# A fused recurrence and MLP kernel: the up product of four token chunks at once in 512 columns, running sums, and the mean of w_out taken off late

## Chip, cores, metric

One core of one Trainium2 chip. The metric is the device time of one execution in microseconds (us); a quoted time is the median of several executions.

## The reference, cut to what matters

A gated linear recurrence (4 batches, 8 heads, 768 steps, head size 48) makes 3072 token rows of 384; an MLP with d_ff = 1024 follows:

```python
# for each batch and head, over t
state = alpha[t][:, None] * state + outer(k[t], v[t])
y[t] = q[t] @ state
# x: (3072, 384) from y
h = x @ w_in                                  # (3072, 1024)
solu = h * softmax(h)
ln = (solu - mean(solu)) / sqrt(var(solu) + 1e-6) * g_ln
out = ln @ w_out                              # (3072, 384)
```

The weights come in float64, so the kernel also converts them. The kernels work without softmax's division: with u = h * exp(h), the layer norm cancels the scale but for the small epsilon, which needs the sum of exp and the sum of u squared of each token.

## The kernel before

Tokens are taken in chunks of 128. Four chunks, one per batch, make a group (128 steps of the recurrence); there are six groups. Attention of a group: `scores` (two halves, each into four PSUM banks), `masked` (DVE empties the banks), `read_state` and `read_values` (the product y), `next_state`. MLP of a chunk: `up`, `partial`, `down`, `finish`.

```python
def scores(g, half, a=None):
    a = a or banks("a", [NP, P])              # the same four PSUM banks each time
    ...
def masked(half, batches=range(B)):
    for b in batches:
        nc.vector.tensor_tensor(out=sT[:, b, ...], in0=a[b], in1=mask..., op=ALU.mult)

def up(n, half):                              # one chunk, half of d_ff
    h = ps_h.tile([P, HF, P], FP, tag="h", name="h")
    for f in range(HF):
        for a in range(KC):
            nc.tensor.matmul(h[:, f], lhsT=w_in[:, a, ...], rhs=d["xT"][:, a], ...)   # 128 columns
    nc.scalar.activation(out=d["e"][:, fs], in_=h, func=AF.Exp)
    nc.vector.tensor_tensor(out=d["u"][:, fs], in0=h, in1=d["e"][:, fs], op=ALU.mult)
    nc.scalar.activation(out=d["u2"][:, fs], in_=d["u"][:, fs], func=AF.Square)

for m in range(B, N + 1):                     # one chunk per turn
    ...                                       # up(m), a part of the next group's attention
        if s == 2:
            scores(g, 0); masked(0)
    ...
        if s == 3:
            read_begin(); read_state(0); read_state(1)
        if fall:
            down(m - 1, 0)                    # one chunk behind up
        if s == 3:
            read_state(2); read_state(3)
        if fall:
            down(m - 1, 1)
    ...
        if s == 2:
            scores(g, 1); masked(1)
```

## Time and profile before

| | before |
|---|---|
| median time | 430.35 us (428.69 to 430.63) |
| span of the profiled run | 427.6 us |
| mean granted clock of TensorE | 0.963 |
| stage A, to the first `up` of group 1 | 136.5 us |
| loop 1 (group 1's `up`, attention of group 2) | 57.1 us |
| three steady groups | 59.2, 59.0, 57.3 us |
| group 5 without attention, last `down`, tail | 44.0, 5.4, 9.1 us |

The stages are cut at the starts of `h` products in TensorE's timeline.

### The profile page before, as it was taken

How to read it: one execution, taken by the hardware profiler on the slowest of the kernel's cores; microseconds unless marked ns; L12 is line 12 of the kernel's file. 1: busy time of each engine (PE TensorE's matmuls, PEld its weight loads, DVE VectorE, ACT ScalarE, POOL GpSimd, SP SyncE). 2: the span in 40 equal slices, each digit the busy share in tenths (PEclk: the TensorE clock that was granted, in tenths of full speed). 3: DMA queues.
4: the chain of work that ended last, by engine and by line, in shares of the span. 5: the costliest groups of instructions: out<-in, count | busy, mean ns of one | idle time of the engine just before them, and what ended most of it. 6: DMA issues, size and time to landing. Idle time of an engine off the chain costs nothing.

```text
span 427.6 us, 12193 instructions
## 1 busy us (share of the span) xinstructions
PE 390.4 (91%) x5401; PEld 318.0 (74%) x5401; DVE 277.2 (65%) x480; ACT 144.3 (34%) x276; POOL 129.4 (30%) x142
## 2 busy tenths in 40 slices
PE   8667998598788989999999999999999999999992
PEld 8466897154667867878897797779788977977761
DVE  2869876899472998746976819976559863133331
ACT  0362776731105215252060522242420512222220
POOL 4100000004410566202772207561128723033330
PEclk9767999898899999999999999999999999999997
DMA  9976299530441933102844006651015000000010
GB/s 174 181 103 187 76 240 181 61 75 19 106 81 35 154 56 75 40 4 37 132 94 94 21 3 97 128 118 32 3 33 63 18 20 23 2 21 18 20 37 28
DMA packets 82047, 30.90 MB, mean 72 GB/s; under 512 B 60473, under 2 KB 80193, under 8 KB 81985
## 3 DMA queue, kind: packets, MB, share of 16 engines
q1 hardware_dynamic: 81536, 29.90, 35.4%
q8 instruction: 44, 0.72, 0.7%
q10 hardware_dynamic: 448, 0.14, 0.2%
q14 instruction: 19, 0.15, 0.1%
HBM read 25.30 MB, written 4.72 MB: 70 GB/s over the span
## 4 chain that ended last, share of the span: by engine, by line
PE 69%; DVE 16%; SPq 4%; DMA 4%; ACT 3%; issue 2%; ACTq 0%; POOL 0%; DVEq 0%
PE o L398 25%; PE h L346 24%; PE y L283 10%; PE a L251 5%; PE kv L325 2%; DMA raw<-in_moe_w_in_dram 2%; DVE aT L189 2%; SPq L138 2%; DVE u L352 2%; PE o L404 2%; SPq L160 1%; DVE low L497 1%; DVE top L493 1%; ACT w_out L516 1%; PE tp L270 1%
## 5 line engine op out<-in xcount | busy, mean ns | idle before, releaser
L346 PE MATMUL h<-xT,w_in 128*128 128x128 f32 x1152 | 135.4, 277 | 0.8 <-DVE u L352 0.7
L398 PE MATMUL o<-w_out,u 128*128 128x385 f32 x384 | 132.7, 496 | 2.7 <-ACT o_sb L426 2.1
L346 PEld LDWEIGHTS h<-xT,w_in 128*128 128x128 f32 x1152 | 130.8, 192 | 4.3 <-DVE u L352 1.5
L398 PEld LDWEIGHTS o<-w_out,u 128*128 128x128 f32 x384 | 71.3, 192 | 50.5 <-issue 3.1
L352 DVE TENSOR_TENSOR u<-h,e 128x512 f32<-128x512 f32 x48 | 33.1, 690 | 62.7 <-ACT e L351 62.7
L424 POOL TENSOR_TENSOR r<-sums,mhalf 128x1 f32<-128x1 f32 x24 | 13.3, 553 | 147.4 <-DVE sums L420 147.4
L351 ACT ACTIVATE e<-h 128x512 f32<-128x512 f32 x48 | 28.5, 593 | 84.0 <-PE h L346 83.9
L353 ACT ACTIVATE u<-u 128x512 f32<-128x512 f32 x48 | 30.2, 630 | 74.1 <-DVE u L352 74.1
L212 POOL TENSOR_TENSOR kT<-kT,hT 128x1024 f32<-128x1024 f32 (+1 forms) x10 | 18.4, 1859 | 89.0 <-DVE kT L164 89.0
L262 DVE TENSOR_TENSOR sT<-a,mask 128x512 f32<-128x512 f32 x44 | 27.5, 683 | 17.4 <-PE a L251 17.4
L361 POOL TENSOR_TENSOR part_e<-e 128x512 f32<-128x512 f32 x20 | 30.1, 1506 | 14.0 <-ACT e L351 14.0
L251 PE MATMUL a<-qv,kT 32*128 32x128 f32 x704 | 27.0, 301 | 5.8 <-DVE least L202 3.2
L251 PEld LDWEIGHTS a<-qv,kT 32*128 32x128 f32 x704 | 24.7, 209 | 7.6 <-issue 4.0
L426 ACT ACTIVATE o_sb<-o,r 128x384 f32<-128x384 f32 x24 | 14.0, 582 | 44.4 <-POOL r L424 44.4
L283 PE MATMUL y<-sT,vn 128*32 128x128 f32 x768 | 24.5, 284 | 2.7 <-issue 2.6
L313 ACT COPY xT<-y 128x384 f32<-128x384 f32 x24 | 11.4, 479 | 43.5 <-PE y L283 43.5
L189 DVE TENSOR_TENSOR_SCAN aT<-aT,seed 128x516 f32<-128x516 f32 x18 | 25.3, 1407 | 0.6
L283 PEld LDWEIGHTS y<-sT,vn 128*32 128x32 f32 x768 | 21.7, 114 | 4.0 <-issue 3.2
L334 DVE TENSOR_TENSOR state<-state,kv 128x512 f32<-128x512 f32 x8 | 5.5, 687 | 25.9 <-PE kv L325 25.9
L361 DVE TENSOR_TENSOR part_u<-u 128x512 f32<-128x512 f32 x20 | 15.0, 749 | 11.1 <-ACT u L353 11.1
L189 DVE TENSOR_TENSOR_SCAN hT<-aT,unit 128x516 f32<-128x516 f32 x18 | 20.9, 1214 | 0.1
L283 PE MATMUL y<-qv,state 32*32 32x128 f32 x1280 | 19.0, 278 | 1.6 <-issue 1.6
(114 smaller groups left out, 456.3 us busy)
## 6 DMA issues: line engine op xcount, KB each, us to landing
an<-in_alpha_dram SPq DMA_DIRECT2D x24, 192.0 KB, 5.1
kn<-in_k_dram SPq DMA_DIRECT2D x24, 192.0 KB, 4.6
qn<-in_q_dram SPq DMA_DIRECT2D x24, 192.0 KB, 4.6
out_dram<-o_sb SPq DMA_DIRECT2D x24, 192.0 KB, 1.9
vn<-in_v_dram SPq DMA_DIRECT2D x24, 128.0 KB, 3.6
raw<-in_moe_w_out_dram SPq DMA_DIRECT2D x8, 384.0 KB, 3.9
raw<-in_moe_w_in_dram SPq DMA_DIRECT2D x16, 128.0 KB, 4.4
vn<-in_v_dram SPq DMA_DIRECT2D x24, 64.0 KB, 3.5
```

Of the source, the lines that this page charges most:

```text
L189: nc.vector.tensor_tensor_scan(out=o, data0=a, data1=s, initial=1.0, op0=ALU.mult, op1=ALU.add)
L212: nc.gpsimd.tensor_tensor(out=kT[:, part], in0=kT[:, part], in1=hk[:, part], op=ALU.mult)
L251: nc.tensor.matmul(a[b][:, i], lhsT=kT[quarter(b), kb], rhs=qv[quarter(b), qb], start=kb == h, stop=kb != h, tile_position=(32 * b, 0), sk ...
L262: nc.vector.tensor_tensor(out=sT[:, b, half * NP : half * NP + NP], in0=a[b], in1=mask[:, None, :].to_broadcast([P, NP, P]), op=ALU.mult,)
L283: nc.tensor.matmul(y_bank(b)[quarter(r), a], lhsT=lhsT, rhs=rhs, start=(b, r) not in begun, stop=stop, tile_position=(row, 32 * r), skip_g ...
L346: nc.tensor.matmul(h[:, f], lhsT=w_in[:, a, (f0 + f) * P : (f0 + f + 1) * P], rhs=d["xT"][:, a], start=(a == 0), stop=(a == KC - 1),)
L351: nc.scalar.activation(out=d["e"][:, fs], in_=h, func=AF.Exp)
L352: nc.vector.tensor_tensor(out=d["u"][:, fs], in0=h, in1=d["e"][:, fs], op=ALU.mult)
L353: nc.scalar.activation(out=d["u2"][:, fs], in_=d["u"][:, fs], func=AF.Square)
L361: eng.tensor_tensor(out=t, in0=d[key][:, 0:HF], in1=d[key][:, HF:FC], op=ALU.add)
L398: nc.tensor.matmul(o[:, 0 : DM + 1], lhsT=d["u"][:, f], rhs=w_out[:, f], start=(f == 0), stop=(f == FC - 1), skip_group_check=True,)
L426: nc.scalar.activation(out=o_sb, in_=d["o"][:, 0:DM], func=AF.Copy, scale=r)
```

## The change

The intent: `up` of a group's four chunks as one product of 512 columns, so 48 records per group where there were 48 per chunk, and a quarter of the weight loads; sums over d_ff as running adds of 512 columns instead of trees; sums over partitions by small products in 32-column squares; the mean of w_out is no longer subtracted before the first `down`, but added to the output for group 0 and taken off w_out on POOL during group 1. Since `u` of a group is complete only after eight steps, `down` trails `up` by a whole group. The core of the diff:

```diff
-    def up(n, half):
-        ...
-                nc.tensor.matmul(
-                    h[:, f], lhsT=w_in[:, a, (f0 + f) * P : (f0 + f + 1) * P], rhs=d["xT"][:, a],
+    def up(g, f):
+        h = ps_h.tile([P, T4], FP, tag="h", name="h")
+        for a in range(KC):
+            nc.tensor.matmul(
+                h, lhsT=w_in[:, a, f * P : (f + 1) * P], rhs=d["x"][:, a].rearrange("p b t -> p (b t)"),
...
+    def running(g, f):
+        for i, eng in enumerate((nc.gpsimd, nc.vector)):
+            p = d["p"][:, i]
+            eng.tensor_tensor(out=p, in0=d[0][i] if f == 1 else p, in1=d[f][i], op=ALU.add)
...
+    def centre(f):
+        nc.gpsimd.tensor_tensor(out=w_out[:, f, 0:DM], in0=w_out[:, f, 0:DM], in1=mean_sb, op=ALU.add)
...
+    todo = [(3, 0), (3, 1)]
+    for g in range(1, G + 1):
+        for s in range(FC):
+            if rise:
+                up(g, s)
...
+                elif s == 6:
+                    masked(0)              # first scores were issued in step 5
...
+            if rise and s:
+                running(g, s)
...
+            if todo:
+                n, half = todo.pop(0)
+                down(n, half)              # chunks of the group before
+            if more:
+                if s == 5:
+                    scores(g + 1, 0)
+                elif s == 6:
+                    scores(g + 1, 1)
+                elif s == 7:
+                    masked(1)
+                    read_begin()
+                    for i in range(4):
+                        read_state(i)
+                    read_values(g + 1)
+                    next_state(g + 1)
```

The first stage is rebuilt as well: the weights come in eight pieces into slots that later hold `u`, alpha of group 0 is transposed on TensorE, and ScalarE checks the range of pieces 2 and 3 ahead of the first exp.

## The prediction

> **What bounds the kernel now.** I read the page first, then the chain of waits in order of time, then busy time by stretches, then the timeline of one group of four chunks. From the page (busy tenths in 40 slices, then two rows of the costliest groups):
>
> ```profile
> PE   8667998598788989999999999999999999999992
> DVE  2869876899472998746976819976559863133331
> L346 PE MATMUL h<-xT,w_in 128*128 128x128 f32 x1152 | 135.4, 277 | 0.8 <-DVE u L352 0.7
> L398 PE MATMUL o<-w_out,u 128*128 128x385 f32 x384 | 132.7, 496 | 2.7 <-ACT o_sb L426 2.1
> ```
>
> TensorE (PE) is full from slice 16 on, some 160 us into the span; before that VectorE (DVE), the weight conversion and the loads share the limit. Each fp32 matmul is two records (576 products, 1152 records). The stretches show it as one row each (length, PE busy, weight-load busy, DVE, ACT, POOL):
>
> ```profile
> 48.00:84.00 36.00, 28.80 (x398) 23.67 (x396) 26.68 (x54) 26.80 (x69) 0.00 (x0) 0.95 0.76 155
> 136.00:160.00 24.00, 22.13 (x176) 18.81 (x165) 21.95 (x27) 6.59 (x12) 12.25 (x10) 1.00 0.64 107
> 193.65:252.84 59.19, 59.19 (x893) 48.96 (x893) 41.71 (x67) 19.42 (x33) 24.16 (x25) 1.00 0.35 69
> ```
>
> The last row is a steady group: 59.2 us, PE never idle, full clock. What it is made of stands in the chain (start, us, what):
>
> ```profile
> 193.65 5.56 PE h L346 x48
> 199.21 5.19 PE o L398 x16
> 204.73 5.46 PE h L346 x48
> ...
> 217.09 5.36 PE h L346 x48
> 222.45 2.00 PE a L251 x64
> 224.45 5.38 PE o L398 x16
> 230.17 2.00 PE a L251 x64
> 232.17 5.55 PE h L346 x48
> ...
> 247.30 3.63 PE y L283 x128
> 250.93 1.91 PE kv L325 x96
> ```
>
> Each chunk's `up` is 48 records, each `down` 16, and between `o` and the next `h` 0.33 us go by (204.40 to 204.73): the two small sum products of L404. Between the two `a` blocks lie 5.7 us of other PE work, and the timeline shows what they hide:
>
> ```profile
> 225.50 2.48 DVE L262 TENSOR_TENSOR sT<-a,mask 128x512 f32<-128x512 f32 x4
> 232.18 2.48 DVE L262 TENSOR_TENSOR sT<-a,mask 128x512 f32<-128x512 f32 x4 [2.82 <-PE a L251]
> 235.14 0.60 ACT L351 ACTIVATE e<-h 128x512 f32<-128x512 f32 x1 [8.88 <-PE h L346]
> 235.77 0.69 DVE L352 TENSOR_TENSOR u<-h,e 128x512 f32<-128x512 f32 x1 [1.10 <-ACT e L351]
> 236.49 0.63 ACT L353 ACTIVATE u<-u 128x512 f32<-128x512 f32 x1 [0.76 <-DVE u L352]
> ```
>
> Emptying the four banks of scores costs DVE 2.5 us, and it starts at once because nothing stands ahead of it.
>
> [...] 5.46/48 = 114 ns for 128 columns, 5.19/16 = 324 ns for 385, a slope of 0.82 ns per column and little fixed cost. So wide columns buy little. [...] in the trace the loads of `h` are about 113 ns each, hidden but just as long as the 128-column product. [...] the trace has the 256-column partial sums of DVE at 0.42 us alone and 1.28 us beside POOL[...].
>
> **The change part by part, steady group.**
> - `up`: 48 records of 512 columns, 324 + 127 x 0.82 = 428 ns each, 20.6 us, against 5.56 + 5.46 + 5.36 + 5.55 = 21.9. Gain 1.3 us per group.
> - Sums: four gaps of 0.33 go (1.3 us); sixteen small column-tiled matmuls of 64 columns come, 32 records at 28 ns (3.63/128 of `y`) = 0.9 us. Gain 0.4.
> - DVE and POOL trees become seven adds of 512 (0.75 and 1.5 us each): 5.3 against 9 us on DVE, 10.5 against 12 on POOL. Off the path, worth nothing by themselves.
> - Work left on PE: `up` 20.6, `down` 8 x 2.6 = 20.8, attention 14.6 (transposes 1.4, scores 4.0, read 7.3, new state 1.9), sums 0.9, switching 0.6: 57.5 against 59.1.
> - **Order**, from the instruction order of the built kernel. Attention of the next group is squeezed into eight steps. Step 6 is up, down (5.2 us), then the second scores, which want the four banks of the first scores back. On DVE their masking now stands behind that step's `u`: after the end of `up` come exp 0.6, `u` 0.7, three small operations 0.6 and masking 2.5 = 4.4 us, with only a `down` of 2.6 to hide it: PE waits 1.8. Step 7 is worse: masking stands behind the last running sum too: 0.6 + 0.7 + square 0.6 + add 0.8 + 2.5 = 5.2 against 2.6: PE waits 2.6 before the read. The first scores wait about 0.6 more on ScalarE (the split queries, then three copies of 0.5). Together 5 us: a steady group of 62.5 for 59.2.
>
> **Stage by stage.**
> A, to the first `up` of group 1 (before: about 136). The three first loads are all in 192-byte pieces and land near 20.2 as now. Values are issued behind 32 weight transfers instead of 16, at about 37, so the first read begins near 40 (now 36.8). ScalarE must then check pieces 2 and 3 before the first exp; their 32 issues at 0.42 to 0.54 us end near 50, landing 3 to 4 us later, so `u` of step 0 is at about 57. Then PE has six `up` at 2.6 and eight array sums at 4 x 0.43 = 1.7 us (no longer four in parallel, 13.8 against 6.3 us in all): 29 us, to 86. DVE goes on from the last `u` (about 83): 2.5 + 2 x 4.1 of conversion, group 1's transposes and scans 15, finishes 2, queries and POOL 5 to about 115, then scores, masks, read and state 18.5: A = 133. Centring (3.8 us on DVE now) is off this path.
> B, loop of group 1, with only one chunk's `down` to fill in. DVE before the first scores: wait 3.2, four `u` 3, transposes 3 x 3.1, scans 9, sums 2.3, finish 1.1 = 28, then POOL and ScalarE 5: 33; after it 2 + 2.6 + 3.9 + 2 + 2.6 + 5.2 + 7.3 + 1.9 = 27.5. B = 60, with PE work of 41.
> C, three steady groups: 187.5. D, group 5 without attention: 20.6 + 20.8 + 1 = 42.5. E, the last four chunks' `down`, which now trail by a whole group: 21.8. Tail as now: 427.6 less 418.5 = 9.
> Sum 133 + 60 + 187.5 + 42.5 + 21.8 + 9 = 454 of span, and 2.7 more for the measured median (430.35 against 427.6) gives 457. I take off 4, since hand scheduling stacks waits: **453 us**.
>
> **The rivals.** (1) The waits at steps 5 to 7 don't bind, because masks get in earlier than I count, and the start is as short as its lighter DVE work suggests. For: conversions shrink from 70 operations to 40, and centring leaves DVE. Then C loses 15, A perhaps 8: 430, about the same. Against: the order on DVE is fixed in the build. (2) B overlaps too, with PE at its work of 41: then PE-bound throughout, some 412 to 418, faster. Against: DVE rows in the start of B add up to 28 us before any score. (3) Loads bind longer, ScalarE's check of piece 3 stalls the first exp past 60, and clocks fall in the gaps of A and B: 465 to 470. For: the row of 37 to 48 us has a granted clock of 0.84.
>
> **Range and chances.** The trailing `down` (E with PE idle in B, some 18 us) I hold nearly certain, the waits in C likely (four fifths), A is good to 8 us either way. Range 432 to 468. Faster by over 2% needs nearly all idle time gone: 0.06; within 2% needs half of it gone: 0.14; slower 0.80.
>
> **What would show it.** Right: records of `h` with 512 columns near 430 ns back to back; a steady group of 61 to 64 us, with PE idle 1 to 3 us before the second scores and before the read, released by the masking on DVE; group 1's loop near 60 us with PE busy about 41; a last stretch of only `down`, 21 us; first exp after 50 us. Wrong: a steady group under 59 us with PE full, or group 1's loop under 50, or a first stage under 125 us.

## More of the kernel before

The lines that show what bounds it are in the prediction. One more row of the page matters later: the clock granted to TensorE in 40 slices of the span, in tenths (9 is 90% or more).

```profile
PEclk9767999898899999999999999999999999999997
```

After the first stage the clock is at 90% or more in every slice until the tail.

## The result, and the profile after

502.68 us (501.21 to 503.66, 4 runs) against 430.49 us (428.69 to 431.47): a ratio of 1.168, 95% interval 1.163 to 1.173. A ratio is always the mean time of one kernel's runs over the mean of the other's runs of the same rounds, so it is not quite the ratio of the medians. Executions over 1.5% slower than the fastest of the same kernel are left out of the means. Slower was predicted, but the time lies far above the range of 432 to 468.

| stage | before | predicted | after |
|---|---|---|---|
| A, to first `up` of group 1 | 136.5 | 133 | 150.6 |
| B, loop 1 | 57.1 | 60 | 71.2 |
| C, three steady groups | 175.5 | 187.5 | 207.1 |
| D, group 5 without attention | 44.0 | 42.5 | 42.6 |
| E, last `down` | 5.4 | 21.8 | 21.6 |
| tail | 9.1 | 9 | 8.4 |
| span | 427.6 | 454 | 501.6 |

D, E and the tail are right within 0.6 us. A, B and C together are 48 us over. Busy tenths and clock of the kernel after, from its page:

```profile
PE   9738399584889818699989899898899897999993
PEclk9879599797789977799989899988999998999998
```

The clock row has dips all along, in the steady groups too, where the kernel before had none. Two rows of the costliest groups (count, busy us, mean ns, idle before):

```profile
L350 PE MATMUL h<-x,w_in 128*128 128x512 f32 x288 | 136.2, 611 | 9.6 <-DVE slot L357 9.6
...
L256 PE MATMUL a<-qv,kT 32*128 32x128 f32 x704 | 40.2, 343 | 26.1 <-POOL qv L232 17.0
```

The wide product costs what the 1152 narrow records of before cost (135.4 us there). The scores, though not touched by the change, went from 27.0 to 40.2 us busy. The stretches (length, PE busy, weight loads, DVE, ACT, POOL, then the granted clock) of loop 1, a steady group, and the last `down`:

```profile
150.80:221.83 71.03, 51.05 (x685) 31.68 (x685) 39.47 (x48) 17.96 (x30) 30.30 (x25) 0.86 0.25 49
...
291.18:360.73 69.55, 63.90 (x765) 38.90 (x765) 41.14 (x60) 19.97 (x33) 22.61 (x20) 0.95 0.28 58
...
471.60:493.24 21.64, 21.59 (x96) 12.56 (x96) 2.68 (x15) 2.33 (x4) 2.20 (x4) 1.00 0.10 37
```

A steady group has 63.9 us of PE "busy" for work that the prediction put at 57.5. So the work itself was slower, and that shows in TensorE's timeline (start, us, what, idle before it and who released it):

```profile
319.14 2.74 PE L350 MATMUL h<-x,w_in 128*128 128x512 f32 x6
321.72 2.76 PE L423 MATMUL o<-w_out,slot 128*128 128x385 f32 x8
326.66 4.33 PE L256 MATMUL a<-qv,kT 32*128 32x128 f32 x64 [2.18 <-POOL qv L232]
...
336.37 3.75 PE L256 MATMUL a<-qv,kT 32*128 32x128 f32 x64
...
348.15 3.81 PE L288 MATMUL y<-qv,state 32*32 32x128 f32 x184 [0.20 <-DVE sT L267]
352.38 1.08 PE L288 MATMUL y<-qv,state 32*32 32x128 f32 x66 [0.41 <-issue]
353.39 1.95 PE L288 MATMUL y<-sT,vn 128*32 128x128 f32 x62
355.83 2.04 PE L288 MATMUL y<-sT,vn 128*32 128x128 f32 x65 [0.49 <-issue]
...
359.56 1.17 PE L330 MATMUL kv<-vn,kg 128*32 128x64 f32 x34 [0.79 <-issue]
```

The waits stand where the prediction had them: before the first scores on the queries, inside the second scores (3.75 us for 2.0 of work, at a clock of 1.00: it is fed bank by bank as the masks empty them), and before the read on `sT`. Three things the prediction did not have: the first scores take 4.33 us after their wait, 184 records of the read take 3.81 us, and there are gaps called "issue", in which TensorE waits for nothing that the profile shows (0.41, 0.49 and 0.79 us here). The same table of stretches, for the two slow blocks, gives the cause of the first two:

```profile
326.66:330.90 4.24, 4.24 (x64) 3.84 (x64) 2.40 (x2) 1.72 (x4) 3.58 (x3) 0.60 0.69 160
...
348.10:352.00 3.90, 3.81 (x184) 3.18 (x184) 0.00 (x0) 0.00 (x0) 0.00 (x0) 0.59 0.02 4
```

The granted clock is 0.60 and 0.59; over the 33 us of the same group ahead of the wait it is 1.00. Cut into finer stretches, the clock is 0.50 from 327.8 to 330.2 and from 348.15 to 351.0; with the partly slow slices at the ends, each is by estimate about 3.4 us at half speed (for the first, 4.24 us at 0.60 come to 4.24 x 0.40 / 0.50).

It does not come each time. In the third steady group of the same run the first scores ran at full clock (1.00) behind the same wait:

```profile
396.22 2.71 PE L256 MATMUL a<-qv,kT 32*128 32x128 f32 x64 [2.20 <-POOL qv L232]
```

That group is also the shortest of the three (69.3, 69.5 and 68.2 us).

DVE's side of the waits, in the same group:

```profile
335.54 2.48 DVE L267 TENSOR_TENSOR sT<-a,mask 128x512 f32<-128x512 f32 x4
...
345.01 0.69 DVE L368 TENSOR_TENSOR p<-p,u 128x512 f32<-128x512 f32 x1 [0.70 <-ACT u L358]
345.62 2.48 DVE L267 TENSOR_TENSOR sT<-a,mask 128x512 f32<-128x512 f32 x4
```

The first scores end at 330.99, their masks start 4.6 us later, behind the next `u`; the second masks start after the running sum. That is the order the prediction described.

In stage A, the first exp came at 56.4 and was held by the range check of piece 3, as predicted, and TensorE then ran slowly (clock 0.62 from 57.7 to 62.3):

```profile
57.76 4.54 PE L350 MATMUL h<-x,w_in 128*128 128x512 f32 x6 [9.62 <-DVE slot L357]
```

### The profile page after: what moved, and what is told of

Read it like the earlier page. It is cut to its first block, busy times and chain, and to the rows that moved or that the text cites. A ratio compares the mean times of both kernels' runs of the same rounds, so it can differ in the third digit from the quotient of the medians.

```text
span 501.6 us, 10779 instructions
## 1 busy us (share of the span) xinstructions
PE 417.8 (83%) x4705; PEld 250.4 (50%) x4705; DVE 262.2 (52%) x410; ACT 147.0 (29%) x251; POOL 127.7 (25%) x124
## 4 chain that ended last, share of the span: by engine, by line
PE 40%; DVE 24%; issue 4%; ACT 3%; POOL 2%; DMA 1%; SPq 0%; DVEq 0%; ACTq 0%; POOLq 0%
PE h L350 12%; PE o L423 10%; PE y L288 9%; PE a L256 6%; DVE sT L267 4%; DVE aT L193 4%; DVE p L368 3%; DVE hT L193 3%; DVE slot L357 3%; PE kv L330 2%; DVE kT L168 2%; ACT e L356 2%; POOL qv L232 1%; DVE least L207 1%; POOL qe L232 1%
## 5 line engine op out<-in xcount | busy, mean ns | idle before, releaser
L350 PE MATMUL h<-x,w_in 128*128 128x512 f32 x288 | 136.2, 611 | 9.6 <-DVE slot L357 9.6
L423 PE MATMUL o<-w_out,slot 128*128 128x385 f32 x384 | 136.7, 503 | 3.6 <-DVE o_mean L441 3.6
L423 PEld LDWEIGHTS o<-w_out,slot 128*128 128x128 f32 x384 | 74.3, 196 | 61.2 <-issue 20.8
L350 PEld LDWEIGHTS h<-x,w_in 128*128 128x128 f32 x288 | 54.3, 195 | 72.9 <-issue 51.9
L357 DVE TENSOR_TENSOR slot<-h,e 128x512 f32<-128x512 f32 x48 | 33.0, 688 | 110.0 <-ACT e L356 110.0
L256 PE MATMUL a<-qv,kT 32*128 32x128 f32 x704 | 40.2, 343 | 26.1 <-POOL qv L232 17.0
L358 ACT ACTIVATE u<-slot 128x512 f32<-128x512 f32 x48 | 30.3, 630 | 65.5 <-DVE slot L357 65.5
L368 POOL TENSOR_TENSOR p<-p,e 128x512 f32<-128x512 f32 x30 | 40.1, 1336 | 33.0 <-ACT e L356 32.8
L368 DVE TENSOR_TENSOR p<-p,u 128x512 f32<-128x512 f32 x30 | 30.3, 1011 | 8.4 <-ACT u L358 8.4
L288 PEld LDWEIGHTS y<-qv,state 32*32 32x32 f32 x1280 | 22.0, 126 | 22.7 <-DVE sT L267 15.6
```

Of the source, the lines that this page charges most:

```text
L256: nc.tensor.matmul(a[b][:, i], lhsT=kT[quarter(b), kb], rhs=qv[quarter(b), qb], start=kb == h, stop=kb != h, tile_position=(32 * b, 0), sk ...
L288: nc.tensor.matmul(y_bank(b)[quarter(r), a], lhsT=lhsT, rhs=rhs, start=(b, r) not in begun, stop=stop, tile_position=(row, 32 * r), skip_g ...
L350: nc.tensor.matmul(h, lhsT=w_in[:, a, f * P : (f + 1) * P], rhs=d["x"][:, a].rearrange("p b t -> p (b t)"), start=(a == 0), stop=(a == KC ...
L357: nc.vector.tensor_tensor(out=u, in0=h, in1=e, op=ALU.mult)
L358: nc.scalar.activation(out=u2, in_=u, func=AF.Square)
L368: eng.tensor_tensor(out=p, in0=d[0][i] if f == 1 else p, in1=d[f][i], op=ALU.add)
```

## The experiments

Theory after the result: (a) a longer wait of TensorE can cost twice, once as the wait and once as slower work behind it, because the granted clock falls (0.60 and 0.59 in the two blocks above, 1.00 over the 33 us ahead of the first); (b) long unbroken runs of narrow records end in issue gaps (0.41 to 0.79 us above); (c) `down` trailing by a group leaves idle time in loop 1 and 21.6 us alone at the end. The rivals: the wide product itself is slow; the start is to blame; what is repaired in one place is lost in the next.

### e1: masks issued right behind their scores

```diff
                 if s == 5:
                     scores(g + 1, 0)
+                    masked(0)
                 elif s == 6:
                     scores(g + 1, 1)
+                    masked(1)
                 elif s == 7:
-                    masked(1)
                     read_begin()
```
(and the old `masked(0)` of step 6 goes)

> The changed kernel with one thing moved: each masking of the four score banks is issued right behind its scores, ahead of the next step's u and running sum on DVE. Theory (the waits at steps 6 and 7 come from the order on DVE[...]): the waits of 1.7 and 2.7 us before the second scores and the read vanish in the three steady groups, the read's first half goes from 3.8 back to 1.9 us, so a steady group falls from 69.5 to about 63, group 1's loop from 71 to about 63, the whole from 502.7 to about 475 us. Rival (the masks only expose the next wait, u and the running sum being late instead): a steady group stays above 67, the whole above 492.

Measured 479.79 us, ratio 1.114 (1.106 to 1.121); 475 was expected. Steady groups fell from 69.0 on average to about 65. The second scores take 2.07 us again and the read starts at once at a clock of 1.00; what stays is the wait before the first scores, with slow scores (clock 0.59) behind it, and a longer gap in the read:

```profile
312.34 4.23 PE L256 MATMUL a<-qv,kT 32*128 32x128 f32 x64 [2.18 <-POOL qv L232]
...
333.46 1.08 PE L288 MATMUL y<-qv,state 32*32 32x128 f32 x66 [1.51 <-issue]
```

So the order of the masks on DVE was worth 23 us: 12 in the three steady groups, and 10 in loop 1, which ends after 61.2 us instead of 71.2. In the steady group shown the two mask waits came to 4.4 us; with them went the slow clock behind the read's wait (1.1), and the longer issue gap gave 1.1 back.

### e2: products on constants in front of the three waits

```diff
+                    warm(40 if g == 1 else 9, ps_h, "h")
                     scores(g + 1, 0)
...
+                    warm(14 if g == 1 else 7, ps_h, "h")
                     scores(g + 1, 1)
...
+                    warm(18 if g == 1 else 11, ps_h, "h")
                     read_begin()
```

> The changed kernel with throwaway 128-column products of ones put into PE's waits before the first scores, the second scores and the read (9, 7 and 11 of them in a steady group; 40, 14 and 18 in group 1's loop). They shorten no wait. Theory[...]: the scores after the wait go from 4.3 to about 2.1 us and the read's first half from 3.8 to about 1.9, a steady group from 69.5 to about 65.5, group 1's loop from 71 to about 63, whole about 482 us, mean granted clock of the stretches 1.00. Rival (scores and read are slow after a wait for another cause, such as their operands or small tiles): nothing but added work, 500 to 508 us.

Measured 498.19 us, ratio 1.159: most of the expected gain was missed. The fillers did their work where they stood (first scores 2.69 instead of 4.33 us), but the read, now without a pause in front of it, ran into a longer issue gap, and the clock fell there:

```profile
347.25 1.05 PE L288 MATMUL y<-qv,state 32*32 32x128 f32 x62 [1.80 <-issue]
348.23 5.37 PE L288 MATMUL y<-sT,vn 128*32 128x128 f32 x128
```

The clock in the stretch of the second line was 0.68, and the block takes 3.70 us in the kernel before. Behind the gap of 1.51 us in e1 the clock stayed at 1.00. Filling all waits alike moved the loss here; it did not remove it.

### e3: range checks of pieces 2 and 3 behind the first exps

```diff
-    in_range(2)
-    in_range(3)
...
         if f % 2:
+            if p < 4:
+                in_range(p)
```

> The changed kernel with ScalarE's range checks of weight pieces 2 and 3 moved behind the first exps of group 0. Theory (the first exp, at 56.4 us, waits on ScalarE behind a check that waits for piece 3 to land at 54.5): first exp near 46 us, the first up of group 1 at about 141 instead of 150.6, whole about 493 us. Rival (conversion on DVE waits for the same piece anyway): the first exp moves but the end of the first stage by less than 3 us, whole 499 to 503.

Measured 494.05 us, ratio 1.148: as expected, 8.6 us less. The first exp comes at 45.2 us, and the first `up` of group 1 starts at 143.5 instead of 150.6 (141 was expected), and the steady groups stay at 69.

### e4: the wide product cut into four of 128 columns

```diff
-        for a in range(KC):
-            nc.tensor.matmul(h, lhsT=w_in[:, a, ...], rhs=d["x"][:, a].rearrange("p b t -> p (b t)"), ...)
+        for b in range(B):
+            for a in range(KC):
+                nc.tensor.matmul(h[:, b * P : b * P + P], lhsT=w_in[:, a, ...], rhs=d["x"][:, a, b], ...)
```

> The changed kernel with each up of 512 columns done as four products of 128 columns, all else alike: undoes the width alone. Theory (width is worth 0.15 us a step, 48 steps, less what lies in waits): 3 to 7 us slower than the changed kernel, about 507. Rival (narrow products are bound by their weight loads, so width is worth more): 515 or more. Rival (width is worth nothing on the path): within 1 us.

Measured 506.61 us, ratio 1.180 (1.171 to 1.188). By the medians that is 3.9 us slower, as expected, but it is not clear of the spread: the runs overlap (503.28 to 509.82 against 501.21 to 503.66), and the two profiled runs have nearly the same span (501.4 and 501.6 us). The trace shows the width itself: an `up` with its `down` takes 5.27 us from one to the next in this form and 5.17 us in the wide one. Over 46 steps 0.1 us would be some 4 us, by estimate; in the profiled run it was made up in the steady groups, where the waits before the first scores are shorter (1.83 to 1.90 us) and two of the three were not followed by slow scores. The wide product is not what made the kernel slow: without it the kernel is no faster.

### e5: e1, and the read split around the last `down`

```diff
+            if more and s == 7:
+                read_begin()
+                read_state(0)
+                read_state(1)
             if todo:
                 n, half = todo.pop(0)
                 down(n, half)
...
                 elif s == 7:
-                    read_begin()
-                    for i in range(4):
-                        read_state(i)
+                    read_state(2)
+                    read_state(3)
```

> The kernel with early masks (e1), and besides the read of the old state split in two around the down of step 7, as the kernel before has it. Theory (the gaps marked 'issue', 1.5 us after some 190 records of the read in a row and 0.5 us twice later[...]): the 1.5 us gap goes, a steady group falls from 65 to 62 to 63.5 us, the whole from 479.8 to about 472. Rival (the gaps belong to the read's operands or banks, wherever it stands): same gaps, 478 to 482.

Measured 472.95 us, ratio 1.100 (1.092 to 1.108): as expected. This is how the kernel before had it. The two halves of the read:

```profile
321.77 1.90 PE L288 MATMUL y<-qv,state 32*32 32x128 f32 x128
...
326.40 1.91 PE L288 MATMUL y<-qv,state 32*32 32x128 f32 x128
```

No gap is left inside them; in e1 the same 256 records had a gap of 1.51 us after the 190th. In the sums of waits "y on issue" falls from 10.1 us in e1 to 4.1.

Where the gaps fall can be counted. In the group of the changed kernel shown above, 66 + 62 = 128 records of TensorE lie between the gap at 352.38 and that at 355.83. Counted over the timelines of all runs from 40 us on, after the first such gap each "issue" gap (0.2 to 1.9 us) lies 128 records behind the one before it, or a multiple of 128 less at most five. So the gaps come at a count of records, not at a certain length of run; by that count e5 has a point in the second half of the read too, and with the `down` shortly before it no gap shows there. No run isolated what makes the gaps; why they come is not shown.

### e6: e1, and the state's decay on POOL moved from step 3 to step 6

```diff
-                    decay(g + 1)          # step 3, ahead of the queries on POOL
...
                     scores(g + 1, 1)
                     masked(1)
+                    decay(g + 1)          # step 6
```

> The kernel with early masks (e1), and besides the decay of the state on GpSimd (4.1 us in step 3, beside the scans on DVE) put off to step 6. Theory (PE's wait of 2.2 us before the first scores, and the half clock of those scores after it, come from the scans and sums on DVE and the queries on GpSimd being drawn out by each other): the second pass of scans falls from 8.0 to about 6 us, the wait goes, the scores take 2.1 instead of 4.2 us, a steady group falls from 65 to about 61.5, the whole to about 468. Rival (the wait is DVE's own row of work, GpSimd has nothing to do with it): wait stays above 1.5 us, 477 to 481.

Measured 471.76 us, ratio 1.095; 468 was expected. The wait before the first scores halves, and the clock holds at 1.00:

```profile
307.31 2.68 PE L256 MATMUL a<-qv,kT 32*128 32x128 f32 x64 [1.05 <-POOL qv L232]
```
```profile
306.20:310.00 3.80, 2.74 (x66) 2.38 (x65) 0.91 (x3) 2.81 (x6) 3.72 (x4) 1.00 0.82 198
```

The clock is 1.00 in that stretch, 0.59 in e1's (312.3 to 316.5). Taking 1.1 us from the wait took 1.6 us more from the scores behind it (e1's line of the same group is shown there). This is the clearest pair for point (a): same records, same order on TensorE, 4.23 against 2.68 us. The second scans of that group on DVE took 1.97, 1.23 and 1.23 us; in the changed kernel, with the decay still in step 3, 1.97, 1.39 and 2.04.

### e7: all repairs together

e5 and e6 and e3; values loaded ahead of the second weight piece; ScalarE's copies of the array sums ahead of one weight piece's work; group 1's keys turned back before `finish` and decay in stage A; one more chunk's `down` moved from stage A to loop 1, and chunk 1's moved next to the scores of stage A; its read split, with four fillers between the halves; POOL's subtraction of the mean later in loop 1. So its gain in stage A is that of several edits together.

```diff
-    down(1, 0)
...
-    todo = [(3, 0), (3, 1)]
+    todo = [(2, 0), (2, 1), (3, 0), (3, 1)]
...
-            if p > 3:
+            if p == 4:
                 scaled(p)
                 in_range(p)
...
     array_sums(0, FC - 1)
+    scaled(5)
+    in_range(5)
```

> All mends of the changed kernel at once: early masks, split read, late decay, late range checks (e3), values loaded ahead of the second weight piece, the copies of the array sums and the transposed keys ahead of the slower ScalarE work behind which they stood, and the down of chunk 2 moved into group 1's loop, where PE idles. Theory (waits by order, and the clock they cost, are nearly all of the loss but the trailing group of downs): steady groups of about 60, first stage near 125, group 1's loop near 60, the last group's down still 21.6: 440 to 450 us, so still slower than before. Rival (width and sums in themselves cost something): above 460.

Measured 457.36 us, ratio 1.061 (1.055 to 1.068); 440 to 450 was expected. Stage A takes 140.6 us, loop 1 61.3, the steady groups 60.6, 60.7, 60.5. So 45 of the 72 us are repaired, and 27 stay.

### e8: the kernel before, with the mean of w_out never taken off

```diff
-        nc.scalar.activation(out=o_sb, in_=d["o"][:, 0:DM], func=AF.Copy, scale=r)
+        nc.vector.scalar_tensor_tensor(
+            out=o, in0=mean_sb, scalar=s[:, 0:1], in1=d["o"][:, 0:DM], op0=ALU.mult, op1=ALU.add
+        )
+        nc.scalar.activation(out=o_sb, in_=o, func=AF.Copy, scale=r)
...
-    centre(m)
```

> One part of the change alone, on the kernel before: the mean of w_out is never taken off the weights; each chunk's output gets mean times column sum added on DVE instead (0.6 us each, 24 times, where DVE has slack). Theory (centring is 3.8 us of DVE on the path between conversion and group 1's scans, and the only part of the change that shortens the path): 3.5 to 5 us faster, about 426. Rival (the scans wait for other things anyway, or the added DVE work delays finishes): within 1.5 us of 430.

Measured 425.05 us, ratio 0.987 (0.981 to 0.994): as expected, and the fastest version. (The gain is clear of noise, but under the 2% from which a run is called faster.) DVE's timeline shows why. In the kernel before, the first scans of group 1 (second line) stand behind 3.81 us of subtraction and the wait for the mean:

```profile
86.63 3.81 DVE L543 TENSOR_TENSOR w_out<-w_out,mean 128x384 f32<-128x384 f32 x8 [0.25 <-PE mean L538]
90.35 3.47 DVE L189 TENSOR_TENSOR_SCAN hT<-aT,unit 128x516 f32<-128x516 f32 x3
```

In e8 the same scans start at 84.16, and the first `up` of group 1 moves from 136.5 to 130.6. So keeping the mean off the path of the first stage is a gain of 1.3% by itself. This is not quite the part that the change has: there the mean is taken off w_out later, on POOL; here it never is.

### e9: e5, with fillers before the first scores only

```diff
                 if s == 5:
+                    warm(40 if g == 1 else 9, ps_h, "h")
                     scores(g + 1, 0)
```

> The kernel with early masks and split read (e5), and throwaway 128-column products in the one wait that is left in a steady group, the 2.2 us before the first scores (9 of them; 40 in group 1's loop). The cost of the clock by itself[...]. Theory (a wait of about 2 us halves the granted clock over the scores after it): the first scores fall from 4.2 to 2.1 to 2.7 us, a steady group from 63.1 to about 61.3, group 1's loop by some 4 us, the whole from 473 to about 464. Rival (scores slow for another cause): a steady group stays within 0.5 of 63.1, the whole 472 or more.

Measured 472.84 us: the total did not move, against an expected 464. The steady groups did as expected (61.3 to 61.7 us instead of 63.2, first scores 2.67 us). In loop 1 the 40 fillers had to wait for their own PSUM bank and then ran past the moment at which the queries were ready:

```profile
180.03 12.10 PE L392 MATMUL warm<-ones 128*128 128x128 f32 x80 [6.00 <-DVE slot L357]
```

The scores started at 192.06 instead of 183.50, and loop 1 took 64.1 us instead of 60.6.

### e10: e7, with group 2's scans back in stage A

```diff
     read_state(3)
+    alpha_T(2)
+    alpha_over(2)
...
     next_state(1)
+    for i in range(3):
+        scan_back(2, i)
```

> All mends (e7), and besides the transposes and first scans of group 2's decays done behind group 1's masks in the first stage, as the kernel before has them, where DVE idles, instead of in group 1's loop. Theory (group 1's loop is DVE's row of work from its first u to the queries, so PE idles there whatever the order of its own work): the loop falls from 61.3 to about 55, the first stage grows by less than 1, the whole from 457.4 to about 451. Rival (the loop is bound by GpSimd's keys, decay and queries): it stays above 59.

Measured 457.67 us against an expected 451: no gain. Loop 1 takes 60.2 us for 61.3 (55 was expected, above 59 the rival), the first `up` of group 1 starts at 141.74 instead of 140.60, and TensorE's wait for the queries in loop 1 is the same (7.05 against 7.04 us). My reason, that the scans sat on loop 1's chain, was wrong; what that wait hangs on was not isolated.

### e11 and e12: the kernel before, uncentred, with parts of the changed start

e11 issues `up` of group 0 ahead of the weight conversions that follow it; e12 adds the changed kernel's order of loads and alpha transposed on TensorE.

```diff
-    convert(6)
     up(0, 1)
-    convert(7)
+    convert(6)
     up(1, 1)
+    convert(7)
```

> The kernel before with the mean never taken off the weights (e8), and besides each up of group 0 issued ahead of the conversion it stood behind, so that its exp does not queue on ScalarE behind the scaling of that piece. From the trace of before: eight rounds of 4.3 us between 48 and 84 us in which DVE idles 1.2 us for exp. Expected 0.6 to 0.9 us less per round: about 420 us against 425 for e8. If the rounds are bound by ScalarE's sum of work instead, 424 to 426.

> e11 with the start of the changed kernel besides: decays loaded first in token order and transposed on TensorE, keys and queries loaded ahead of the weights. In the changed kernel the queries were ready at 21.9 us, in the one before at 30.2. Expected: the first read starts at about 33 us instead of 36.8, 2 to 4 us less in all, about 417 us. If the conversions on DVE bind from there on, no gain over e11.

Measured 428.18 and 429.74 us against expected 420 and 417: slower than e8 by 3 and 5 us, and the same as the kernel before (ratios 0.997 and 0.999). In e11 the last array sums wait 5.62 us for a ScalarE copy of the sums before, so that the mean is ready 4 us later than in e8 (87.5 against 83.7), and the first `up` of group 1 starts at 133.4 instead of 130.6; in e12 at 138.9. Neither of these two parts of the rebuilt start helps the kernel before.

### e13: the kernel before, with `down` trailing by four chunks

```diff
-    hid = pool("hid", 4)
+    hid = pool("hid", 5)
...
-    for m in range(B, N + 1):
+    for m in range(B, N + 4):
-        rise, fall = m < N, m > B
+        rise, fall = m < N, m >= B + 4
...
-            down(m - 1, 0)
+            down(m - 4, 0)
```

> The kernel before with its down trailing four chunks behind its up instead of one (five hidden buffers instead of four); nothing else is changed, and the work of TensorE is the same. Theory: the 27 us by which the mended changed kernel is still above the kernel before come from the trailing, since loop 1 then has no down to put into its waits and the last four chunks' down (4 x 5.2 us) stand alone at the end: the last group grows by three chunks' down, 15.6 us, and loop 1 doesn't shrink by as much because its attention chain binds; total about 443 to 448[...]. Rival: the trailing is free (loop 1 shrinks by what the end grows), and the 27 us come from the wide products and their order: total within 4 us of before.

Measured 441.08 us; one of the four runs (445.45 us) was slow, the fast ones took 438.68, 441.06 and 441.10. Ratio 1.024 (1.015 to 1.033): clear of no change, on both sides of 2%. It is the direction of the theory, 10 us by this ratio and 11.6 by the medians, against the expected 13 to 18 and against the rival's 4 at most. The stretches of e13: loop 1, a steady group, and the `down` at the end:

```profile
136.23:188.46 52.23, 40.90 (x816) 38.09 (x813) 43.12 (x54) 18.70 (x31) 21.72 (x21) 0.93 0.37 63
188.46:247.50 59.04, 59.04 (x894) 48.82 (x892) 41.35 (x63) 18.95 (x32) 23.41 (x24) 1.00 0.34 66
...
407.82:430.27 22.45, 22.45 (x82) 13.83 (x81) 2.56 (x16) 2.33 (x4) 2.20 (x4) 1.00 0.10 35
```

The steady groups are untouched. Loop 1 has no `down` left and shrinks by only 4.8 us (57.1 to 52.2), with 11.3 us of idle TensorE in it; the end grows by 17. Where no `down` breaks the read, issue gaps of 0.46 and 1.50 us come up in this kernel too.

### e14: e9, without the fillers in loop 1

```diff
                 if s == 5:
+                    if g > 1:
+                        warm(9, ps_h, "h")
                     scores(g + 1, 0)
```

> e5 with 9 warm products ahead of the first scores in the steady groups only, none in group 1's loop, where they cost 12 us in e9. Theory: the wait of 2.18 us ahead of the first scores is what sets TensorE to half clock in the steady groups, and filling it saves 1.4 to 1.8 us in each of three of them: 63.1 to about 61.5 per group, total about 468. Rival: e9's total missed because the saving is lost again later in each group, total within 1 us of 473.

Measured 469.89 us, ratio 1.094, against 472.95 for e5. The total falls by 3.1 us, between the two expectations (468 and 473). By the trace, three steady groups and what follows are 5.5 us shorter, and stage A and loop 1, whose instructions are the same in both, ended 2.2 us later in this run (210.0 against 207.8 at the last `kv` run of loop 1). So the filled wait gains what was expected, and e9's total was lost in loop 1.

## Why the prediction was wrong

**Right.** The cost of the wide product (2.58 us from one step to the next in the timeline; predicted 20.6 per eight), `down`, the sums, the first exp at 56 and `u` at 57, the order on DVE and the waits it causes, D, E and the tail. The slower direction and its named structural cause, the trailing `down`: I held "some 18 us" of idle time for nearly certain, and e13 measures 10 to 12 us for it alone. (The costs used came from the slope in the trace, 0.82 ns per column, and held. The 113 ns of a weight load are its busy time over the count, 130.8/1152; one record lasts 192 ns.)

**The step that failed: "Together 5 us: a steady group of 62.5 for 59.2".** It counted each wait as its own length and the work behind it at full clock (1.00). The steady groups measured 69.3, 69.5 and 68.2 us. The group shown is 7.0 us over, of which its timeline gives 6.6: 2.8 us of slow clock (first scores 4.33 against 2.67 in e14; 184 records of the read in 3.81 against 2.71 for 188 in e6), 1.7 us of issue gaps (0.41 + 0.49 + 0.79), 1.5 us of longer waits (2.18 + 1.7 + 2.66 = 6.5 for 5.0, of which the first was taken as 0.6), and 0.6 us by which the first scores exceed 2.0 even at full clock. The three groups together are C's 19.6 us over; the last of them is shorter by 1.3 because its first scores kept the full clock. e1, e5, e6 and e14 each remove one or two of these and gain about what they stood for.

My own rival 3 noted a clock of 0.84 in a stretch with gaps (37 to 48 us of the kernel before), but I did not carry that into the sum. Which waits had slow work behind them is seen across the runs, at the first scores of the steady groups:

| wait before the first scores | runs | scores behind it |
|---|---|---|
| 0.2 to 0.3 us | e14 (3) | 2.66 to 2.67 us |
| 1.05 to 1.15 us | e6 (3), e7 (3) | 2.65 to 2.69 us |
| 1.83, 1.90, 1.86 us | e4 (3) | 2.69, 2.69, 3.79 us |
| 2.16 to 2.25 us | e1 (3), e5 (3) | 3.28 to 4.32 us |
| 2.25, 2.18, 2.20 us | the changed kernel (3) | 3.42, 4.33, 2.71 us |
| 2.21, 2.16, 2.21 us | e3 (3) | 2.71, 3.42, 4.06 us |

From 1.83 to 2.25 us it falls one way or the other: slow in 11 of 15 cases (in 10 of the 12 from 2.16 us on), and the same 2.2 us was once followed by scores of 2.71 us both in the changed kernel (clock 1.00) and in e3. What decides it is not shown. The table is of the first scores only: before the read, waits of 0.87 us and three times 0.20 with only six records among them (2.66 us in all) were followed by the slow clock in all three groups of the changed kernel (182 to 185 records of the read in 3.57, 3.81 and 3.81 us, for 188 in 2.71 in e6; clock 0.59 in the second).

**A = 133.** Measured 150.6. The shape was right. Moving the range check of piece 3 saves 8.6 us (e3), but it is no part of the miss: the prediction had its effect, `u` at 57, and still came to 133, so the 17.6 us lie behind it. By the timeline the array sums end at 90.4 (predicted 86) and the first scores start at 126.0 (predicted 115), after waits of 4.71, 3.59 and 3.60 us on ScalarE and DVE; the clock in that part is 0.81, and 0.79 in the part after it, which takes 24.6 us for the predicted 18.5. Moving the copies and the order (with e3, in e7) brings A to 140.6.

**B = 60.** Measured 71.2: 35.2 us to the first scores (predicted 33) and 36.0 after them (predicted 27.5), at a mean clock of 0.79. So here too it is mostly the second part, where most blocks of the attention follow a wait; e1, with the masks in time, brings loop 1 to 61.2.

**The remaining 27 us of e7** over the kernel before: e13 puts 10 to 12 us on the trailing `down`. Of the 17.1 us between the spans of e7 and e13, the stages give 4.4 to A, 9.1 to loop 1, 6.4 to the steady groups, and 2.8 back at the end. In loop 1 of e7 the wait for the queries (7.04 us) and the slow scores behind it (4.46 us, for 2.67 in e14) are the visible part; e10 failed to move it, so its cause stays open. So does how far the trailing costs the same in the changed order as in the kernel before.

Of the rivals, none came in. Rival 3 (loads and clocks, 465 to 470) named lower clocks, but only in A and B, and as a side effect.

## What to carry to other kernels

Where TensorE is the bound, don't count a wait on it as its own length only: here 11 of 15 waits of 1.83 to 2.25 us had slow scores behind them (3.28 to 4.33 us for 2.7; in the one cut into finer stretches, by that estimate 3.4 us at a clock of 0.50). Try narrow products spread between wide ones: here the read split around a `down` had no gap inside its halves (e5: 472.95 us for the 479.79 of e1). A wider product is worth what its saved records cost (here about 0.1 us a step, some 4 us of 430 by estimate) and must pay for the buffering that it forces: a consumer that trails by a group leaves the first group without filler and the last without company. And a change of many parts is worth taking apart: of the parts tried on the old kernel (the mean, two parts of the start, the trailing `down`), only the one with the mean made it faster (e8, 425.05 us).
